# The order of the setup in a linear-attention and mixture-of-experts kernel

## The chip, the cores and the metric

The kernel runs on one core of a Trainium2 chip. The metric is the device time of one execution in microseconds. TensorE multiplies (and turns matrices), VectorE, ScalarE and GpSimd do elementwise work, SyncE issues most DMAs. Each engine works through its own instructions in order and waits for the others by semaphores.

## The reference

For each of 4 batches and 8 heads (width 48) a linear attention with decay w and a bonus u runs over 768 steps. Its rows of 8 x 48 = 384 then go through a mixture of 8 experts, one per token.

```python
for t in range(S):                                   # S = 768
    kt, vt, rt = (k[:, :, t], v[:, :, t], r[:, :, t])
    cur = np.einsum('bhd,bhe->bhde', u[None] * kt, vt)
    y[:, :, t] = np.einsum('bhd,bhde->bhe', rt, state + cur)
    state = w[None, :, :, None] * state + np.einsum('bhd,bhe->bhde', kt, vt)
...
logits = x @ w_gate + modality_bias[modality_id]     # x: 3072 rows of 384
e_idx = np.argmax(logits, axis=1)                    # gate_w: its softmax probability
h = np.maximum(x[mask] @ w1[e], 0.0)                 # for each expert e, mask = e_idx == e
out[mask] = gate_w[mask, None] * (h @ w2[e])
```

## The kernel before

The attention is cut into 24 units: 6 chunks of 128 steps for each of 4 batches, the batches in the inner order, so units 0 to 3 are the first chunks and have no state behind them. Heads go in 4 pairs of 96 rows. For a unit, `decay` multiplies r with powers of w (tile rc, GpSimd), `keys` multiplies k with inverse powers (kc, VectorE), `scores` multiplies the two on TensorE (32 small products into two banks psc), `causal` masks the two banks (VectorE), `values` multiplies the masked scores with v (py) and makes the state products (pst, kt times v), and `bonus` gives for every row the sum of u, r and k (d, from rk: `own_turned` or `own_keys`), by which `own` scales v (dv, eight activations on ScalarE). `token` adds dv to py, and the rows are scaled, split and turned for the routing. r and k of a unit lie turned in HBM (tile ud, 96 rows; k's half is loaded for some units only). For the units in `TURNED`, k is loaded in rows alone (tile kv) and turned on TensorE (`keys_turned`, tile pkT). `carry` scales k for the state (kt, GpSimd).

The order on every engine is written out by hand: the instructions of an engine run in the order in which `setup` and the loop of `run` name them (`tc.manual_schedule`). PSUM has four banks for scores and turned keys, taken in turn, two for py, one (tag "s") for the state products and the bonus: the state products of a unit can't be written before ScalarE has copied out the state (`state`) and d (`taken`) of the unit before.

`setup` makes powers of w: w (1.5 KB, loaded first by SyncE) is spread on VectorE and summed up by a scan into the table pw; ScalarE and VectorE write powk and powr from it, each in halves. Unit 0's k is multiplied by VectorE in two pieces, r by GpSimd (pairs 0 and 1, one by one) and by VectorE (pairs 2 and 3). Rows 0 to 15 of the tiles ud, kv and kt, and the state tiles, are blanked: ud0 by VectorE, ud1 by GpSimd, ud2, ud3, kt and st[1] by ScalarE. u is loaded into single elements of a tile of 96 x 4 (uT) and copied by GpSimd into ub. wtok holds the decays that `carry` uses: four wk on ScalarE, turned on TensorE. Ten products of ones (pwarm, `WARM`) are issued before the first scores, and three more (`DENSE`) in front of unit 1's scores, whose banks are written over by them. All loads are issued by SyncE. After setup, step 0 of the loop in `run` starts with unit 1's scores; `setup2` (the gate's weights, the biases) is spread over the first steps, one instruction at a time.

Of the kernel before, what the change touches and what calls it, by code (L numbers as in the profile page):

```python
# [49 lines left out]
GROUPED = 6  # L50
# [13 lines left out]
LOW, TOP = 64 - D, 64 + D  # L64
HALVES = slice(0, 64), slice(64, TOP)


class _Kernel:
# [16 lines left out]
    def setup(self):  # L85

        nc, c = self.nc, self.c
        w = c.tile([P, NPR], F32, name="w")
        nc.vector.memset(w, 1.0)
        nc.sync.dma_start(w[LOW:TOP, :], self.wT.rearrange("j d a -> (j d) a"))  # L90
        uT = c.tile([P, NPR], F32, name="uT")
        self.ud = [c.tile([P, 2 * NPR * P], F32, name=f"ud{q}") for q in range(4)]
# [3 lines left out]
        zero = c.tile([P, P // 2], F32, name="zero")  # L96
        nc.vector.memset(zero, 0.0)
        warm = self.warm = c.tile([P, 512], F16, name="warm")
        nc.gpsimd.memset(warm, 1.0)
        self.ones16 = warm[:, :P]  # L100
        for t in self.kv:
            nc.vector.memset(t[:, :LOW], 0.0)
        nc.vector.memset(self.ud[0][:LOW], 0.0)
        nc.gpsimd.memset(self.ud[1][:LOW], 0.0)
        H2 = P // 2
        blank = lambda t: nc.scalar.copy(t.rearrange("p (a z) -> p a z", z=P // 2), zero[: t.shape[0]].unsqueeze(1).to_broadcast([t.shape[0], t.shape[1] // (P // 2), P // 2]))
        self.tables = c.tile([P, 3, NPR, H2 + 1], F32, name="tables")
        wb, one0, pw = (self.tables[:, q] for q in range(3))
# [4 lines left out]
        nc.vector.memset(one0[:, :, 0:1], 1.0)  # L113
        nc.vector.memset(uT, 0.0)
        blank(self.ud[2][:LOW])
        self.turned(0)
        self.turned(1)
        nc.sync.dma_start(uT[LOW:TOP, :], self.u.rearrange("o (a z) -> z (o a)", a=NPR))
        self.lines(1, 0)
# [3 lines left out]
        for i in range(3):  # L123
            self.lines(i, 1)
        wg = c.tile([P, DC * E], F32, name="wgf")
        nc.sync.dma_start(wg, self.wg)
        bias = c.tile([P, 2 * E], F32, name="bias")
        nc.sync.dma_start(bias, self.bias.to_broadcast([P, 2 * E]))
        mod = c.tile([P, 2 * NT // P], I32, name="mod")
        nc.sync.dma_start(mod, self.mod)  # L130
        self.raw_in = wg, bias, mod


        pt = self.ps_a.tile([P, 512], F32, tag="big", name="pwarm")
        for _ in range(WARM):
            nc.tensor.matmul(pt, self.ones16, warm, start=True, stop=True)


        self.ones = c.tile([P, P], F32, name="ones")
        nc.vector.memset(self.ones, 1.0)  # L140
        id32 = self.id32 = c.tile([P, P], F32, name="id32")
        make_identity(nc, id32)
        self.mask = c.tile([P, P], F32, name="mask")
        nc.gpsimd.affine_select(self.mask, self.ones, pattern=[[1, P]], compare_op=ALU.is_gt, fill=0.0, base=0, channel_multiplier=-1)
        self.counts()
        flat = lambda t: t.rearrange("p a z -> p (a z)")
# [14 lines left out]
        p64 = pw[:, :, H2 : H2 + 1].rearrange("p a o -> p (a o)")  # L161
        nc.vector.tensor_mul(self.w128, p64, p64)
        self.ub, self.uw = (c.tile([P, NPR, 2], F32, name=n) for n in ("ub", "uw"))
        self.decay(0, NPR, NPR // 2)
        self.keys(0, 2)
        u = self.ctx_[0]
        nc.vector.tensor_mul(u["rc"][:TOP, NPR // 2 :], u["rT"][:TOP, NPR // 2 :], self.powr[:TOP, NPR // 2 :])
        self.own_turned(0)
        self.decay(1)
        self.scores(0)  # L170
        self.wtok = c.tile([P, NPR, 2 * D], F32, name="wtok")
        wk = []
        for pr in range(NPR):
            t = self.a.tile([P, P], F32, tag="wk", name=f"wk{pr}", bufs=4)
            nc.scalar.activation(t, powk[:, pr, :], AF.Copy, scale=self.w128[:, pr : pr + 1])
            wk.append(t)
        blank(self.ud[3][:LOW])
        for t in self.kt:
            nc.scalar.copy(t[:, :, :LOW], zero[:, : NPR * LOW].rearrange("p (a z) -> p a z", a=NPR))
        pt = self.ps_y.tile([P, 512], F32, tag="y", name="pwk")  # L180
        for pr in range(NPR):
            nc.tensor.transpose(pt[:, pr * P : (pr + 1) * P], wk[pr], id32)
        nc.scalar.copy(self.wtok, pt.rearrange("p (a z) -> p a z", a=NPR)[:, :, LOW:TOP])
        blank(self.st[1].rearrange("p b a e -> p (b a e)"))
# [67 lines left out]
    def counts(self):  # L252

        c, v = self.c, self.nc.gpsimd
        self.onesb = c.tile([P, P], BF16, name="onesb")
        v.memset(self.onesb, 1.0)
        self.id16 = c.tile([P, P], F16, name="id16")
        make_identity(self.nc, self.id16)
        self.tok = c.tile([P, NT // P], I32, name="tok")
# [7 lines left out]
        self.base = c.tile([P, E], F32, name="base")  # L267
        v.tensor_copy(self.base, self.cbase)
        self.line = c.tile([P, 1], F32, name="line")
        v.tensor_copy(self.line, self.tok[:, 0:1])  # L270

# [56 lines left out]

    def turned(self, i):
# [5 lines left out]
        self.nc.sync.dma_start(ud[LOW:TOP, :m], self.pd[b * NCH + c].rearrange("j d n -> (j d) n")[:, :m])  # L335
        self.ctx_.setdefault(i, {}).update( rT=ud[:, :n].rearrange("p (a t) -> p a t", a=NPR), kT=ud[:, n:].rearrange("p (a t) -> p a t", a=NPR))
# [55 lines left out]

    def own_turned(self, i):

        u = self.ctx_[i]
        u["rk"], u["uw"] = self.a.tile([P, NPR, P], F32, tag="rk", name=f"rk{i}"), self.ub
        self.nc.vector.tensor_mul(u["rk"][:TOP], u["kT"][:TOP], u["rT"][:TOP])

    def keys(self, i, n=1):
        nc, a, u = self.nc, self.a, self.ctx_[i]  # L400
        u["kc"] = a.tile([P, NPR, P], F32, tag="kc", name=f"kc{i}")
        for q in range(n):
            s = slice(q * NPR // n, (q + 1) * NPR // n)
            nc.vector.tensor_mul(u["kc"][:TOP, s], u["kT"][:TOP, s], self.powk[:TOP, s])

# [34 lines left out]
    def scores(self, i):  # L440
        nc, u = self.nc, self.ctx_[i]
        u["ps"] = [self.ps_a.tile([P, 512], F32, tag="big", name=f"psc{i}_{j}") for j in range(2)]
        if i == 1:

            for q in range(DENSE // 2):
                nc.tensor.matmul(u["ps"][q % 2], self.ones16, self.warm, start=True, stop=True)

        for pr in range(NPR):
            for q in range(2):
                s = slice(64 * q, 64 * q + 64)  # L450
                for j, r in enumerate(HALVES):
                    nc.tensor.matmul(u["ps"][j][s, pr * P : (pr + 1) * P], u["kc"][r, pr, s], u["rc"][r, pr, :], start=True, stop=True)  # L452
# [712 lines left out]
    def run(self):  # L1165
        nc, tc, m = self.nc, self.tc, self.m
# [233 lines left out]
        i, j = NU - 2, NU - 1  # L1400
# [208 lines left out]
```

## Time and profile before

| | us |
|---|---|
| median of 3 runs | 334.5 |
| lowest, highest | 333.94, 335.64 |
| profiled execution, its own time | 336.65 |
| its span | 334.6 |
| TensorE busy in it | 320.0 (96%) |
| VectorE, ScalarE, GpSimd busy | 213.5, 181.7, 159.7 |

The profile is of one execution; the span runs from its first to its last instruction. Times of rows are microseconds from the start of the span. A timeline row begins with the start and the length of a group of like instructions, which may overlap the next; the instruction's engine, line, operation, tiles (out<-in), shape and number follow, and in brackets the idle time of the engine before it with what ended that. PEld is the load of TensorE's stationary operand, SPq the issuing of DMAs by SyncE.

### The profile page before, as it was taken

The numbers are of one execution on the slowest core, as the hardware profiler recorded it, in microseconds if no ns is written. First come the engines' busy times: TensorE is split into PE (matmuls) and PEld (weight loads), VectorE is DVE, ScalarE is ACT, GpSimd is POOL, SyncE is SP. The second block draws the span as 40 slices with busy tenths as digits, with TensorE's granted clock in tenths as the row PEclk, the third lists the DMA queues.
The fourth block names the chain that finished last, engine by engine and source line by source line (L and its number), as shares of the span: only waits on it lengthen the run. The fifth ranks groups of instructions, "written<-read, shape, count | busy, mean of one in ns | idle before, by whom it ended". The sixth has DMA issues, their size and how long they took to land. (4 is left out here: it accounts for less than half of the span.)

```text
span 334.6 us, 15202 instructions
## 1 busy us (share of the span) xinstructions
PE 320.0 (96%) x5434; PEld 263.5 (79%) x5434; DVE 213.5 (64%) x727; ACT 181.7 (54%) x500; POOL 159.7 (48%) x241
## 2 busy tenths in 40 slices
PE   7999998998999999999999999999999999999992
PEld 2888897898978888797878788886888877777771
DVE  6878985899988988896667422286333332234950
ACT  7898888789655578676422222274222225543820
POOL 8978863967599886554458212203111111111211
PEclk9999999899999999999999999999999999999999
DMA  6879986995579999954246431119512211122110
GB/s 185 244 171 207 204 250 222 293 229 155 126 197 270 267 223 299 275 156 119 78 106 231 156 78 47 47 47 332 121 50 65 50 47 24 47 56 62 37 47 5
DMA packets 58013, 48.71 MB, mean 146 GB/s; under 512 B 42344, under 2 KB 50807, under 8 KB 57712
## 3 DMA queue, kind: packets, MB, share of 16 engines
q1 hardware_dynamic: 54768, 38.63, 47.5%
q0 software_dynamic: 3200, 9.47, 8.2%
q8 instruction: 30, 0.49, 0.7%
q14 instruction: 15, 0.12, 0.1%
HBM read 27.99 MB, written 11.83 MB: 119 GB/s over the span
## 5 line engine op out<-in xcount | busy, mean ns | idle before, releaser
L1067 PEld LDWEIGHTS <-whi 128*128 128x128 f16 x1248 | 72.6, 98 | 3.6 <-issue 0.7
L1076 DVE SCALAR_TENSOR_TENSOR hl<-phb,hh 128x256 f16<-128x256 f32 (+1 forms) x48 | 24.4, 508 | 66.8 <-ACTq L1540 66.8
L1130 PEld LDWEIGHTS <-hh 128*128 128x128 f16 x416 | 39.1, 98 | 25.3 <-ACT hh L1071 1.2
L1067 PE MATMUL phb<-mxT,whi 128*128 128x128 f16 x768 | 50.7, 219 | 0.0
L438 ACT ACTIVATE dv<-kv,d 128x48 f32<-128x48 f32 x172 | 43.0, 325 | 0.0
L1071 ACT ACTIVATE hh<-phb 128x256 f16<-128x256 f32 (+1 forms) x48 | 21.5, 455 | 32.4 <-PE phb L1067 22.9
L1067 PEld LDWEIGHTS <-wlo 128*128 128x128 f16 x624 | 37.8, 98 | 0.0
L1036 POOL TENSOR_TENSOR seenb<-otb,putb 128x1 int32<-128x1 int32 x16 | 4.1, 257 | 63.0 <-ACTq L1540 50.8
L458 DVE TENSOR_TENSOR at<-psc,mask 128x512 f32<-128x512 f32 x48 | 32.5, 681 | 1.5 <-PE psc L452 1.4
L1130 PEld LDWEIGHTS <-hl 128*128 128x128 f16 x208 | 19.8, 98 | 15.7 <-issue 2.5
L366 POOL TENSOR_TENSOR rc<-ud,powr 112x512 f32<-112x512 f32 (+1 forms) x25 | 30.8, 1237 | 0.2
L1027 ACT ACTIVATE otb<-po,fac 128x384 f32<-128x384 f32 x16 | 9.3, 580 | 39.5 <-PE phb L1067 39.5
L452 PE MATMUL psc<-rc,kc 64*64 64x128 f32 (+1 forms) x768 | 28.5, 281 | 1.2 <-POOL rc L366 1.0
L701 POOL DMA_INDIRECT rows<-row,posi x24 | 24.6, 1026 | 10.2 <-issue 3.6
L1067 PE MATMUL phb<-mxT,wlo 128*128 128x128 f16 x384 | 29.3, 219 | 0.0
L1130 PE MATMUL po<-whi,hl 128*128 128x384 f16 x136 | 28.0, 326 | 1.2 <-PEq L1605 0.7
L1130 PE MATMUL po<-whi,hh 128*128 128x384 f16 x136 | 27.7, 326 | 0.6 <-ACT hh L1071 0.4
L489 PE MATMUL py<-kv,at 128*64 128x48 f32 x768 | 27.0, 222 | 1.2 <-issue 1.2
L1067 PE MATMUL phs<-mxT,whi 128*128 128x128 f16 x432 | 27.3, 219 | 0.6 <-issue 0.6
L1130 PE MATMUL po<-wlo,hh 128*128 128x384 f16 x136 | 27.7, 326 | 0.0
L452 PEld LDWEIGHTS psc<-rc,kc 64*64 64x64 f32 (+1 forms) x768 | 21.9, 135 | 6.5 <-issue 2.5
L489 PEld LDWEIGHTS py<-kv,at 128*64 128x64 f32 x768 | 25.3, 138 | 2.1 <-issue 1.8
(292 smaller groups left out, 625.6 us busy)
## 6 DMA issues: line engine op xcount, KB each, us to landing
kv<-in_pt SPq DMA_DIRECT2D x21, 384.0 KB, 4.8
ud<-in_pd SPq DMA_DIRECT2D x14, 384.0 KB, 5.4
raw<-in_w SPq DMA_DIRECT2D x12, 256.0 KB, 5.1
raw<-in_w SPq DMA_DIRECT2D x6, 512.0 KB, 5.2
raw<-in_w SPq DMA_DIRECT2D x2, 1536.0 KB, 6.5
rows<-pad SPq DMA_DIRECT2D x10, 193.0 KB, 3.6
ud<-in_pd SPq DMA_DIRECT2D x10, 192.0 KB, 3.8
rt<-in_pt SPq DMA_DIRECT2D x7, 192.0 KB, 5.2
```

The lines of the kernel that those rows point to most:

```text
L366: nc.gpsimd.tensor_mul(u["rc"][:TOP, s], u["rT"][:TOP, s], self.powr[:TOP, s])
L438: nc.scalar.activation(u["dv"][:, sl], u["v"][:, sl], AF.Copy, scale=u["d"][:, h : h + 1])
L452: nc.tensor.matmul(u["ps"][j][s, pr * P : (pr + 1) * P], u["kc"][r, pr, s], u["rc"][r, pr, :], start=True, stop=True)
L458: nc.vector.tensor_mul(u["at"][:, j * NPR : (j + 1) * NPR, :], u["ps"][j].rearrange("p (q t) -> p q t", q=NPR), self.mask.unsqueeze(1).to_ ...
L489: nc.tensor.matmul(py[t, sl], u["at"][:, j * NPR + pr, t], u["v"][:, sl], start=c == h == 0, stop=h == H - 1, skip_group_check=True)
L701: i = nc.gpsimd.indirect_dma_start(out=self.rows, out_offset=bass.IndirectOffsetOnAxis(ap=u["posi"][:, b : b + 1], axis=0), in_=u["row"][: ...
L1027: self.nc.scalar.activation(ot, po[:, :DM], AF.Copy, scale=gf[:, t : t + 1])
L1036: i1 = nc.gpsimd.tensor_tensor(seen, ot[:, 0:1].bitcast(I32), idx, ALU.add)
L1067: self.nc.tensor.matmul(ph[:, q * P : (q + 1) * P], w[:, c0 : c0 + P], self.xT[:, xq, t * P : (t + 1) * P], start=i == q == 0, stop=i == l ...
L1071: self.nc.scalar.activation(self.hh[:, f0 : f0 + fb, t * P : (t + 1) * P], p3, AF.Relu)
L1076: self.nc.vector.scalar_tensor_tensor(self.hl[:, f0 : f0 + fb, r], p3, 0.0, self.hh[:, f0 : f0 + fb, r], ALU.max, ALU.subtract)
L1130: self.nc.tensor.matmul(po[:, :DM], h[:, f, t * P : (t + 1) * P], w[:, c0 : c0 + DM], start=first, stop=last)
```

## The change

- Unit 0's load of r and k is issued by ScalarE; the others stay with SyncE. The loads of wg, bias and mod go behind unit 3's and 4's.
- u is loaded as four rows of 96 (ux), turned by TensorE (one transpose of four columns) and copied into ub by two copies on ScalarE.
- ud0's rows and kt's are blanked by ScalarE early, ud2's by GpSimd; the blanks of ud3 and st[1] on ScalarE move behind `taken(0)`.
- `first` gives the first products of unit 0 in pieces in another order (VectorE: k of pairs 0 and 1, r of pairs 0 and 1, w128, k of pairs 2 and 3, r of pair 2; GpSimd: r of pair 3), and the first scores go through the pairs in the order 0, 1, 3, 2.
- rk of unit 0 is multiplied by GpSimd, behind unit 1's decay, instead of VectorE.
- `keys(1)` stands between unit 0's two masks; `keys_turned(2)` is in the setup; the bonus of unit 0 comes behind it.
- GpSimd's constants are split: `numbers` early, `masks` behind rk, `counts` behind the carry of unit 1.
- Nine products of ones at the start instead of ten, none in front of unit 1's scores.

```diff
-WARM = 10
+WARM = 9
-DENSE = 6
...
+        self.turned(0, nc.scalar)
+        self.turned(1)
+        ux = c.tile([NPR, TOP], F32, name="ux")
+        self.ub, self.uw = (c.tile([P, NPR, 2], F32, name=n) for n in ("ub", "uw"))
+        nc.gpsimd.memset(ux, 0.0)
+        nc.gpsimd.memset(self.ub, 0.0)
+        nc.sync.dma_start(ux[:, LOW:], self.u.rearrange("o (a z) -> (o a) z", a=NPR))
         for t in self.kv:
             nc.vector.memset(t[:, :LOW], 0.0)
-        nc.vector.memset(self.ud[0][:LOW], 0.0)
         nc.gpsimd.memset(self.ud[1][:LOW], 0.0)
...
-        nc.vector.memset(uT, 0.0)
-        blank(self.ud[2][:LOW])
-        self.turned(0)
-        self.turned(1)
-        nc.sync.dma_start(uT[LOW:TOP, :], self.u.rearrange("o (a z) -> z (o a)", a=NPR))
+        blank(self.ud[0][:LOW])
+        for t in self.kt:
+            nc.scalar.copy(t[:, :, :LOW], zero[:, : NPR * LOW].rearrange("p (a z) -> p a z", a=NPR))
         self.lines(1, 0)
...
-        nc.vector.memset(self.ones, 1.0)
+        nc.gpsimd.memset(self.ones, 1.0)
...
-        self.counts()
+        nc.gpsimd.memset(self.ud[2][:LOW], 0.0)
+        self.numbers()
...
-        nc.vector.tensor_mul(self.w128, p64, p64)
-        self.ub, self.uw = (c.tile([P, NPR, 2], F32, name=n) for n in ("ub", "uw"))
-        self.decay(0, NPR, NPR // 2)
-        self.keys(0, 2)
-        u = self.ctx_[0]
-        nc.vector.tensor_mul(u["rc"][:TOP, NPR // 2 :], u["rT"][:TOP, NPR // 2 :], self.powr[:TOP, NPR // 2 :])
-        self.own_turned(0)
+        self.first(p64)
         self.decay(1)
+        self.own_turned(0, nc.gpsimd)
         self.scores(0)
...
-        blank(self.ud[3][:LOW])
-        for t in self.kt:
-            nc.scalar.copy(t[:, :, :LOW], zero[:, : NPR * LOW].rearrange("p (a z) -> p a z", a=NPR))
+        self.masks()
+        psd = self.ps_s.tile([P, 512], F32, tag="s", name="psd")
+        nc.tensor.transpose(psd[:TOP, :NPR], ux, id32[:NPR, :NPR])
+        for j, r in enumerate(HALVES):
+            nc.scalar.copy(self.ub[r, :, j], psd[r, :NPR])
+        self.keys_turned(1)
         pt = self.ps_y.tile([P, 512], F32, tag="y", name="pwk")
         for pr in range(NPR):
             nc.tensor.transpose(pt[:, pr * P : (pr + 1) * P], wk[pr], id32)
         nc.scalar.copy(self.wtok, pt.rearrange("p (a z) -> p a z", a=NPR)[:, :, LOW:TOP])
+        self.causal(0, 0)
+        self.keys(1)
+        self.causal(0, 1)
+        self.own_turned(1)
+        self.keys_turned(2)
+        self.bonus(0, psd)
+        self.taken(0)
+        blank(self.ud[3][:LOW])
         blank(self.st[1].rearrange("p b a e -> p (b a e)"))
-        nc.gpsimd.memset(self.ub, 0.0)
-        for j, r in enumerate(HALVES):
-            nc.gpsimd.tensor_copy(self.ub[r, :, j], uT[r])
-        self.keys_turned(1)
-        self.causal(0, 0)
-        self.causal(0, 1)
-        self.keys(1)
-        self.own_turned(1)
         self.carry(0)
         self.decay(2)
         nc.gpsimd.tensor_mul(self.uw, self.ub, w.unsqueeze(2).to_broadcast([P, NPR, 2]))
-        pst = self.ps_s.tile([P, 512], F32, tag="s", name="psd")
-        self.bonus(0, pst)
-        self.taken(0)
         self.carry(1)
+        self.counts()
         self.feed(3)
...
+    def first(self, p64):
+
+        nc, u, half = self.nc, self.ctx_[0], NPR // 2
+        u["rc"] = self.a.tile([P, NPR, P], F32, tag="rc", name="rc0", bufs=4)
+        u["kc"] = self.a.tile([P, NPR, P], F32, tag="kc", name="kc0")
+        part = lambda eng, out, x, pw, s: eng.tensor_mul(u[out][:TOP, s], u[x][:TOP, s], pw[:TOP, s])
+        lo, hi = slice(0, half), slice(half, NPR)
+        part(nc.gpsimd, "rc", "rT", self.powr, slice(NPR - 1, NPR))
+        part(nc.vector, "kc", "kT", self.powk, lo)
+        part(nc.vector, "rc", "rT", self.powr, lo)
+        nc.vector.tensor_mul(self.w128, p64, p64)
+        part(nc.vector, "kc", "kT", self.powk, hi)
+        part(nc.vector, "rc", "rT", self.powr, slice(half, NPR - 1))
...
-        if i == 1:
-
-            for q in range(DENSE // 2):
-                nc.tensor.matmul(u["ps"][q % 2], self.ones16, self.warm, start=True, stop=True)
-
-        for pr in range(NPR):
+        for pr in range(NPR) if i else (0, 1, 3, 2):
...
-            if i < GROUPED:
+            if 0 < i < GROUPED:
                 each(i + 2, self.keys_turned)
```

## Rows read from the trace of the kernel before

**Rows 1.** Timeline of TensorE, 0 to 27 us (start, length, group)

```profile
1.38 4.45 PE L136 MATMUL pwarm<-warm 128*128 128x512 f16 x10 [1.38 <-POOL warm L99]
...
6.40 0.45 PE L452 MATMUL psc<-rc,kc 64*64 64x128 f32 x8 [0.56 <-POOL rc L366]
7.25 0.89 PE L452 MATMUL psc<-rc,kc 64*64 64x128 f32 x24 [0.41 <-POOL rc L366]
...
9.09 0.63 PE L413 MATMUL psd<-ub,rk 112*64 112x2 f32 x16
...
10.14 0.81 PE L446 MATMUL psc<-warm 128*128 128x512 f16 x3
10.88 1.10 PE L452 MATMUL psc<-rc,kc 64*64 64x128 f32 x32
...
22.85 1.33 PE L489 MATMUL py<-kv,at 128*64 128x48 f32 x32
24.32 0.58 PE L502 MATMUL pst<-kv,kt 128*64 128x48 f32 x15
```

**Rows 2.** Timeline of ScalarE over the same time

```profile
4.86 0.41 ACT L159 COPY powr<-powk 128x256 f32<-128x256 f32 x1
...
6.35 1.03 ACT L106 COPY ud<-zero 16x1024 f32<-16x1024 f32 x1
7.28 0.68 ACT L179 COPY kt<-zero 128x64 f32<-128x64 f32 x4
...
9.14 1.48 ACT L106 COPY st<-zero 128x1536 f32<-128x1536 f32 x1
10.51 0.17 ACT L421 COPY d<-psd 128x8 f32<-128x8 f32 x1
10.72 1.91 ACT L438 ACTIVATE dv<-kv,d 128x48 f32<-128x48 f32 x8
12.54 0.21 ACT L212 ACTIVATE wgsq<-wgf 128x24 f32<-128x24 f32 x1
...
14.00 0.64 ACT L544 COPY st<-pst 64x192 f32<-64x192 f32 x2 [1.16 <-PE pst L413]
...
23.20 0.32 ACT L229 ACTIVATE wghl<-wgf,wgs 128x24 f16<-128x24 f32 x1 [0.51 <-DVE wgs L318]
...
24.06 0.17 ACT L421 COPY d<-pst 128x8 f32<-128x8 f32 x1
```

**Rows 3.** Timeline of VectorE over the same time

```profile
2.98 0.23 DVE L147 COPY tables<-w 128x256 f32<-128x256 f32 x1
...
4.93 0.76 DVE L404 TENSOR_TENSOR kc<-ud,powk 112x256 f32<-112x256 f32 x2
...
21.83 0.62 DVE L566 SCALAR_TENSOR_TENSOR row<-py,sx,row 128x384 f16<-128x384 f32 x1 [1.73 <-ACT row L562]
...
22.43 0.68 DVE L458 TENSOR_TENSOR at<-psc,mask 128x512 f32<-128x512 f32 x1
```

**Rows 4.** Tenths of a microsecond: busy time by engine, clock, DMA share, GB/s

```profile
2.20:2.30 0.10, 0.10 (x2) 0.09 (x1) 0.10 (x2) 0.10 (x1) 0.10 (x2) 1.00 0.16 4
...
2.50:2.60 0.10, 0.10 (x1) 0.00 (x0) 0.10 (x2) 0.10 (x1) 0.10 (x1) 1.00 2.88 369
```

**Rows 5.** Timeline of SyncE's DMA issues: the loads of units 0 and 1

```profile
1.44 0.88 SPq L335 DMA_DIRECT2D ud<-in_pd  x2
```

**Rows 6.** GpSimd by line and shape, 5.6 to 8.5 us (busy, mean ns)

```profile
L366 POOL TENSOR_TENSOR rc<-ud,powr 112x128 f32<-112x128 f32 x2 | 1.5, 768 | 0.0
L366 POOL TENSOR_TENSOR rc<-ud,powr 112x512 f32<-112x512 f32 x1 | 1.3, 1265 | 0.0
```

**Rows 7.** Timeline of GpSimd: the copy that the change moves

```profile
4.95 0.46 POOL L268 COPY base<-idxf 128x8 f32<-128x8 f32 x1
```

**Rows 8.** Busy time by engine (TensorE first) and granted clock, two later stretches

```profile
53.50:54.75 1.25, 0.08 (x3) 0.03 (x2) 0.00 (x0) 1.25 (x3) 0.00 (x0) 1.00 0.89 325
57.00:61.00 4.00, 4.00 (x59) 3.56 (x60) 2.55 (x10) 3.96 (x13) 3.77 (x5) 0.57 0.80 228
```

More of the change, by code (lines that the diff above doesn't have):

```diff
@@ L90, in setup @@
         nc.sync.dma_start(w[LOW:TOP, :], self.wT.rearrange("j d a -> (j d) a"))
-        uT = c.tile([P, NPR], F32, name="uT")
         self.ud = [c.tile([P, 2 * NPR * P], F32, name=f"ud{q}") for q in range(4)]
@@ L124, in setup @@
             self.lines(i, 1)
[L125 to L131, printed above, removed]
         pt = self.ps_a.tile([P, 512], F32, tag="big", name="pwarm")
@@ L195, in setup @@
         nc.gpsimd.tensor_mul(self.uw, self.ub, w.unsqueeze(2).to_broadcast([P, NPR, 2]))
-        pst = self.ps_s.tile([P, 512], F32, tag="s", name="psd")
-        self.bonus(0, pst)
-        self.taken(0)
         self.carry(1)
+        self.counts()
         self.feed(3)
+        wg = c.tile([P, DC * E], F32, name="wgf")
+        nc.sync.dma_start(wg, self.wg)
         self.turned(4)
+        bias = c.tile([P, 2 * E], F32, name="bias")
+        nc.sync.dma_start(bias, self.bias.to_broadcast([P, 2 * E]))
+        mod = c.tile([P, 2 * NT // P], I32, name="mod")
+        nc.sync.dma_start(mod, self.mod)
+        self.raw_in = wg, bias, mod
+    def first(self, p64):
[10 more added lines that the diff above has]
+        part(nc.vector, "rc", "rT", self.powr, slice(half, NPR - 1))
     def setup2(self):
@@ L254, in counts, with masks @@
         c, v = self.c, self.nc.gpsimd
+        self.base = c.tile([P, E], F32, name="base")
+        v.tensor_copy(self.base, self.cbase)
+        self.line = c.tile([P, 1], F32, name="line")
+        v.tensor_copy(self.line, self.tok[:, 0:1])
+    def masks(self):
+        c, v = self.c, self.nc.gpsimd
         self.onesb = c.tile([P, P], BF16, name="onesb")
@@ L258, in counts, with numbers @@
         make_identity(self.nc, self.id16)
+    def numbers(self):
+        c, v = self.c, self.nc.gpsimd
         self.tok = c.tile([P, NT // P], I32, name="tok")
@@ L266, in counts @@
         self.idx, self.rev, self.cbase = (ci[:, q] for q in range(3))
[L267 to L270, printed above, removed]
     def setup5(self):
@@ L327, in feed, with turned @@
         self.lines(i)
-    def turned(self, i):
+    def turned(self, i, by=None):
         b, c = self.units[i]
@@ L334, in turned @@
         m = n if i in TURNED else 2 * n
-        self.nc.sync.dma_start(ud[LOW:TOP, :m], self.pd[b * NCH + c].rearrange("j d n -> (j d) n")[:, :m])
+        (by or self.nc.sync).dma_start(ud[LOW:TOP, :m], self.pd[b * NCH + c].rearrange("j d n -> (j d) n")[:, :m])
         self.ctx_.setdefault(i, {}).update( rT=ud[:, :n].rearrange("p (a t) -> p a t", a=NPR), kT=ud[:, n:].rearrange("p (a t) -> p a t", a=NPR))
@@ L359, in pace, with decay @@
         self.nc.values_load(ap[:1].bitcast(I32)[:, :1], engines=SP, skip_runtime_bounds_check_because="the value is not used, only the time at which it is there")
-    def decay(self, i, n=1, of=None):
+    def decay(self, i):
         nc, u = self.nc, self.ctx_[i]
         u["rc"] = self.a.tile([P, NPR, P], F32, tag="rc", name=f"rc{i}", bufs=4)
-        for q in range(of or n):
-            s = slice(q * NPR // n, (q + 1) * NPR // n)
-            nc.gpsimd.tensor_mul(u["rc"][:TOP, s], u["rT"][:TOP, s], self.powr[:TOP, s])
+        nc.gpsimd.tensor_mul(u["rc"][:TOP], u["rT"][:TOP], self.powr[:TOP])
     def carry(self, i):
@@ L391, in own_keys, with own_turned, keys @@
         nc.gpsimd.tensor_mul(u["rk"][:TOP], u["rc"][:TOP], u["kc"][:TOP])
-    def own_turned(self, i):
+    def own_turned(self, i, by=None):
         u = self.ctx_[i]
         u["rk"], u["uw"] = self.a.tile([P, NPR, P], F32, tag="rk", name=f"rk{i}"), self.ub
-        self.nc.vector.tensor_mul(u["rk"][:TOP], u["kT"][:TOP], u["rT"][:TOP])
-    def keys(self, i, n=1):
+        (by or self.nc.vector).tensor_mul(u["rk"][:TOP], u["kT"][:TOP], u["rT"][:TOP])
+    def keys(self, i):
         nc, a, u = self.nc, self.a, self.ctx_[i]
         u["kc"] = a.tile([P, NPR, P], F32, tag="kc", name=f"kc{i}")
-        for q in range(n):
-            s = slice(q * NPR // n, (q + 1) * NPR // n)
-            nc.vector.tensor_mul(u["kc"][:TOP, s], u["kT"][:TOP, s], self.powk[:TOP, s])
+        nc.vector.tensor_mul(u["kc"][:TOP], u["kT"][:TOP], self.powk[:TOP])
     def bonus(self, i, pst):
```

## The prediction

> **What bounds the kernel now.** I read the table of slices first: TensorE is busy in nine tenths or more of nearly all of them, only the first slice and the last are thinner. So a setup that lets TensorE start earlier should shorten everything behind it, if TensorE is what the next microseconds wait for. That is not visible in a mean, so I read the timeline of TensorE over the first 27 us, then those of ScalarE and VectorE beside it.
>
> TensorE [rows 1]: ten products that write nothing useful fill 1.38 to 5.83. The first scores start at 6.40 and again at 7.25, each time released by GpSimd's decayed r, and end at 8.14. Then it runs on without a gap (transposes, the bonus products at 9.09, three more idle products at 10.14, unit 1's scores at 10.88). From these rows alone the setup is bound by the road to the first scores.
>
> ScalarE [rows 2] tells another story. It waits once, 1.16 us, until the first state is there at 14.00, and from there it works without a gap until it waits 0.51 for VectorE at 23.20: copies of state, the scalings by d, the squares, and pieces of the second setup. At 24.06 it copies d of unit 3 out of the one bank of the state products, which ends at 24.23; TensorE's next group into that bank starts at 24.32, though its group before (22.85) would have let it go on earlier: it took 1.33 us, spread out. VectorE shows the same dependence [rows 3]: it stands still for 1.73 us until ScalarE's row at 21.83, and only then does unit 3's second mask (22.43, done 23.1) come, which TensorE's group of 22.85 needs for its odd heads. So by 24 us TensorE has been caught up by ScalarE and VectorE. A lead won at 8 us is worth something at 24 us only if ScalarE's chain starts earlier too. That chain goes back through 14.00 to d of unit 0 and to what ScalarE does next to it.
>
> **The change part by part.**
>
> *Road to the first scores.* The chain starts with w: VectorE copies it at 2.98, works up the powers, and has kc of unit 0 from 4.93 on (two pieces, 0.76) [rows 3]; ScalarE writes the last quarter of the powers for r at 4.86 to 5.27 [rows 2]. Taking a blank of 16 rows from VectorE (1.03 for the like one on ScalarE, [rows 2]) gains little: w's bytes moved until 2.3 [rows 4], so it lands between 2.3 and 2.98, and ScalarE now starts with a load's issue (0.44, half of SP's two, [rows 5]) and has the four small blanks of kt (0.68, [rows 2]) ahead of the powers too, where it waited before. Bounds: 0.1 gained to 0.3 lost; I take 0, since the powers' last piece hangs on VectorE's, and that on w. Then VectorE's first piece of rc (as long as one of kc, 0.4) ends at about 5.7 and pairs 0 and 1 start at 5.8 instead of 6.40; pair 3 needs GpSimd's single piece (0.77 beside a busy VectorE, [rows 6]: 5.3 to 6.1) and the second kc (6.25); pair 2 the last rc (6.45). The scores end at about 6.95 instead of 8.14: 1.2 us of lead. GpSimd must reach its piece by 5.3: before, everything ahead of the copy at 4.95 was done by then [rows 7]; the change adds a blank of 16 rows (about 1) and takes out three small operations of the masks there and the two copies behind it, so it gets there between 4.95 and 5.95, and I take 5.3.
>
> *Between the two scores.* Before, unit 1's scores started 10.88 − 8.14 = 2.74 after the first ended, the last 0.74 (10.14 to 10.88) being the three products that write nothing. Without them TensorE has four groups of transposes and the bonus (0.63, [rows 1]). But the bonus needs rk of unit 0, and that product moves from VectorE to GpSimd, behind decay(1): both are 112x512 products of 1.27 [rows 6], the first stretched by about 0.2 while VectorE reads the same memory. 6.1 + 1.45 + 1.27 = 8.8. So the bonus runs 8.85 to 9.45, and unit 1's scores start at 9.4 to 9.5: TensorE leads by 1.4 to 1.5 there. keys(1) between the two masks, the transposes of u (one of four columns in place of a small DMA of single elements, GpSimd's two copies and a memset) and the later wg, bias and mod cost nothing: VectorE has its third product of that stretch done at about 9.0, ScalarE waits for the bonus anyway, and wg is first read at 12.54 [rows 2], some 6 us after its new issue. The one warm product less (0.43) lies in time in which TensorE waits.
>
> *Where the lead goes.* After the change ScalarE's order is: d of unit 0, blank of ud3, blank of st, the eight scalings of unit 0, the square of wg, then the state copies that stood at 14.00. Before, both blanks were done ahead of d. From start to next start [rows 2]: d 0.2 (10.51 to 10.72), ud3's blank 0.93 (6.35 to 7.28), st's blank 1.37 (9.14 to 10.51), scalings 1.82 (10.72 to 12.54), the square 0.2 to 0.3. Sum 4.5 to 4.6. With the bonus ending at 9.45, d starts at about 9.55, and the state copies at 9.55 + 4.55 = 14.1, against 14.00 now. The 1.16 us in which ScalarE waited are filled by blanks that stood where it had to wait for something else anyway (new waits: about 0.6 for w128, which now comes behind the first rc, so the four wk start at 5.9; 0.6 for wk's transposes; 0.9 for the bonus). Behind 14.00 ScalarE's and VectorE's order is the old one and has no room, so the second mask of unit 3 (22.43) and d of unit 3 (24.06) come 0.1 later than now, and TensorE, ahead by 1.4 us until then, waits at unit 3's values for 1.5 us and goes on at 24.32 + 0.1. GpSimd, which now has rk of unit 0 (1.27) and the two copies (0.46 and less, [rows 7]) behind its first pieces, is up to 1.2 later from 13 us on; TensorE, which would meet it, is itself held until 24.4.
>
> *The load of unit 0 on ScalarE's queue.* Until now w was alone: unit 0's bytes began at 2.5, w's had moved by 2.3 [rows 4]. Now unit 0's 384 KB are issued by an engine with nothing ahead of them, some 0.6 before the 1.44 of [rows 5], and their first bytes come at about 1.9, ahead of w's. From below: w is not disturbed, 0. From above: w waits until they are through, at the 0.9 that they take beyond 2.3 (384 KB from 1.9 at some 300 GB/s, an estimate below the 369 of [rows 4], end at 3.2). I take 0.1, because w is only 1.5 KB; every microsecond of it goes through powers, rk, bonus and d to ScalarE's chain one to one. *By the Trainium skill (DMA: Bandwidth & Descriptors, "Queues, rings and completion order") the queues of SP and ACT share the same 16 DMA engines, which take turns between them by whole packets, and a completion signal lands only behind all earlier writes of its engine, whatever the queue; by that rule w's signal comes behind whatever of unit 0 is already on its way, a few tenths, and the sum would be 0.3 to 0.5 worse than mine. No row of the trace before shows two such queues at once.*
>
> **The sum.** Profiled execution: 336.65 us, of which the span is 334.6; the median of the other runs is 334.5. Change at 24.3 us: +0.1 (ScalarE's chain) + 0.1 (w) = +0.2; behind it the work and its order are the old ones, so the end moves by as much: 336.85 in the profiled frame, 334.7 against the median.
>
> **The rivals.**
>
> *The lead is kept (gain).* If the state copies at 14.00 come earlier than I work out, because GpSimd's rk is ready by 8.2 and the blanks run shorter beside idle neighbours, or if TensorE is held by something at 24 us that moves with it. For it: 1.4 us of lead at unit 1's scores. Against it: the rows at 21.83 to 24.32. It gives 334.5 − 1.5 = 333.0, and 332.4 if the first scores get the full 1.9 of the gaps and idle products together.
>
> *TensorE's clock falls (slower).* My forecast makes TensorE wait about 1.5 us in one piece at 21.7 to 23.2. The trace has one such place [rows 8]: TensorE was busy 0.08 of 1.25 us from 53.50, and from 57 to 61 its granted clock is 0.57 of full in the mean, so for most of that at the lower of its two levels, 1.2 instead of 2.4 GHz. That is 0.43 x 4 = 1.7 us of its work lost. Before the change nothing of that length stands ahead of 50 us. [...] The price is 1.7 at most, and 1.1 if a third of it falls into waits that TensorE has anyway: 335.8 to 336.4.
>
> *w comes late.* With 0.6 to 0.9 in place of 0.1, everything from the powers on is later and 335.2 to 335.5 results. This is the rival of the shared queues above. For it: w's chain has no slack; against it: its size.
>
> **How the numbers follow.** What a measurement of this kernel can tell from no change is about 0.5%, 1.67 us (333.94 to 335.64 before). Chances: ScalarE's chain unchanged 0.47 (334.7, from 333.9 to 335.5), lead kept 0.25 (333.0), clock falls 0.18 (336.0), w late 0.10 (335.3). Faster than 332.83: half of the second and some of the first's edge, 0.19. Slower than 336.17: four tenths of the clock case, edges of the others with it, 0.14. Between: 0.67. Range for 8 in 10: 332.8 to 336.4, which reaches into the kept lead at one end and to the upper price of the clock at the other.
>
> **What would show it.** Right: first scores at 5.8, unit 1's scores at 9.4 to 9.5, no idle products, but ScalarE's state copies at 14.0 to 14.3, both blanks between d and the scalings, a new wait of TensorE of over 1 us ahead of 23.2, and its state products of unit 3 still at about 24.4. Wrong: state copies of unit 0 before 13.4, or TensorE's unit 3 ended by 23.5 (the lead is kept); VectorE's copy of w later than 3.3 (the queue); a granted clock of one half between 23 and 30 us (the clock).

## The result and the profile after

The changed kernel takes 338.67 us (median of 6 runs, 337.72 and up) against 334.72 of the kernel before: 1.011 of its time, interval 1.0085 to 1.0136. By that ratio it is slower by 3.7 us (2.8 to 4.6). The forecast was no change. Comparisons below use undisturbed executions only, so a median over all runs can lie above what a ratio says; the trace of experiment 7 is disturbed, and only its first 4 us are read.

The profiled execution takes 337.72 us with a span of 335.7. That is only 1.1 over the span of before: from unit 3's state products to the end it takes 307.7, before's 310.3, which has a lower clock at 57 to 61 us [rows 8] where this one has none. So I compare by landmarks in the first 30 us, not by spans.

VectorE of the changed kernel, then GpSimd, from 4.4 us on (columns as in [rows 1]):

```profile
4.44 0.29 DVE L143 COPY tables<-w 128x256 f32<-128x256 f32 x1 [2.58 <-DMA w<-in_wT]
...
7.12 0.42 DVE L212 TENSOR_TENSOR w<-tables 128x4 f32<-128x4 f32 x1
7.47 0.41 DVE L207 TENSOR_TENSOR kc<-ud,powk 112x256 f32<-112x256 f32 x1
7.80 1.36 DVE L207 TENSOR_TENSOR rc<-ud,powr 112x128 f32<-112x128 f32 x1
```

```profile
6.84 0.69 POOL L207 TENSOR_TENSOR rc<-ud,powr 112x128 f32<-112x128 f32 x1 [1.99 <-ACT powr L155]
7.49 1.53 POOL L385 TENSOR_TENSOR rc<-ud,powr 112x512 f32<-112x512 f32 x1
8.97 1.32 POOL L416 TENSOR_TENSOR rk<-ud 112x512 f32<-112x512 f32 x1
```

and the DMA engines in three half microseconds (last column GB/s):

```profile
1.50:2.00 0.50, 0.50 (x2) 0.17 (x2) 0.28 (x2) 0.50 (x1) 0.50 (x1) 1.00 0.60 90
2.00:2.50 0.50, 0.50 (x2) 0.15 (x1) 0.00 (x0) 0.50 (x1) 0.50 (x3) 1.00 0.66 180
2.50:3.00 0.50, 0.50 (x2) 0.15 (x1) 0.00 (x0) 0.49 (x2) 0.42 (x4) 1.00 0.82 328
```

Unit 0's bytes move from 1.84 us on (the first row is empty up to there; the forecast was 1.9), at 180 GB/s until 2.5; before, there was next to nothing at 2.2 [rows 4]. VectorE stands still for 2.58 us until w is there and copies it at 4.44; before, it was busy until 2.98 and did not wait [rows 3]. Its last piece, a quarter of r, takes 1.36 and ends at 9.16, just behind GpSimd's product of 7.49 (9.02). TensorE follows:

```profile
1.39 4.02 PE L131 MATMUL pwarm<-warm 128*128 128x512 f16 x9 [1.39 <-POOL warm L97]
7.26 1.21 PE L464 MATMUL psc<-rc,kc 64*64 64x128 f32 x24 [1.85 <-DVE rc L207]
9.21 0.54 PE L464 MATMUL psc<-rc,kc 64*64 64x128 f32 x8 [0.74 <-DVE rc L207]
...
9.87 1.10 PE L375 MATMUL pkT<-id,kv 128*112 128x128 f32 x4
...
12.60 0.73 PE L430 MATMUL psd<-ub,rk 112*64 112x2 f32 x16
...
26.15 0.32 PE L501 MATMUL py<-kv,at 128*64 128x48 f32 x4 [0.84 <-DVE row L578]
26.81 1.02 PE L501 MATMUL py<-kv,at 128*64 128x48 f32 x28 [0.34 <-DVE wgs L339]
27.97 0.58 PE L514 MATMUL pst<-kv,kt 128*64 128x48 f32 x15
```

Three things are to be seen. TensorE idles 1.85 ahead of the first scores (0.56 before, [rows 1]). The first four transposes behind the scores take 1.10; the like four took 0.66 in the kernel before:

```profile
8.07 0.66 PE L182 MATMUL pwk<-id,wk 128*128 128x128 f32 x4
```

And the landmark of the forecast, unit 3's state products, comes at 27.97 instead of 24.32 [rows 1]: 3.65 later, close to the 3.7 of the runs. The windows (columns as in [rows 4]: TensorE busy first, its clock the last but two) say why the transposes are long:

```profile
9.00:10.00 1.00, 0.79 (x10) 0.51 (x11) 0.30 (x2) 0.00 (x0) 1.00 (x2) 0.72 1.05 309
10.00:11.00 1.00, 1.00 (x6) 1.00 (x7) 0.55 (x1) 0.32 (x2) 0.86 (x4) 0.50 0.94 249
...
12.00:13.00 1.00, 1.00 (x14) 0.66 (x14) 1.00 (x3) 0.34 (x1) 0.58 (x1) 0.57 0.32 65
```

The granted clock is 0.50, the lower of the two levels, from 9.4 to nearly 12.9 us. ScalarE has the order that was forecast:

```profile
13.38 0.17 ACT L438 COPY d<-psd 128x8 f32<-128x8 f32 x1 [1.05 <-PE psd L430]
13.45 1.04 ACT L110 COPY ud<-zero 16x1024 f32<-16x1024 f32 x1
14.39 1.47 ACT L110 COPY st<-zero 128x1536 f32<-128x1536 f32 x1
15.77 1.91 ACT L455 ACTIVATE dv<-kv,d 128x48 f32<-128x48 f32 x8
17.58 0.20 ACT L225 ACTIVATE wgsq<-wgf 128x24 f32<-128x24 f32 x1
...
17.79 0.62 ACT L556 COPY st<-pst 64x192 f32<-64x192 f32 x2
...
27.71 0.17 ACT L438 COPY d<-pst 128x8 f32<-128x8 f32 x1
```

From d to the state copies it takes 4.41 (forecast 4.55), and it works from there to the wait ahead of 26.85 and to unit 3's d as before. So the chain was read rightly; it starts 3.7 late.

### The profile page after: what moved, and what is told of

Its sections match the earlier page's. It is cut to its first block, busy times and chain, and to the rows that moved or that the text cites. A ratio compares the mean times of both kernels' runs of the same rounds, so it can differ in the third digit from the quotient of the medians.

```text
span 335.7 us, 15200 instructions
## 1 busy us (share of the span) xinstructions
PE 318.3 (95%) x5431; PEld 262.4 (78%) x5431; DVE 213.7 (64%) x724; ACT 181.9 (54%) x502; POOL 162.0 (48%) x242
## 5 line engine op out<-in xcount | busy, mean ns | idle before, releaser
L464 PE MATMUL psc<-rc,kc 64*64 64x128 f32 (+1 forms) x768 | 27.7, 276 | 3.2 <-DVE rc L207 2.6
L713 POOL DMA_INDIRECT rows<-row,posi x24 | 25.4, 1057 | 10.3 <-issue 3.3
L385 POOL TENSOR_TENSOR rc<-ud,powr 112x512 f32<-112x512 f32 x23 | 29.7, 1293 | 0.2
L1021 DVE SCALAR_TENSOR_TENSOR wlo<-raw,ws,whi 128x1024 f16<-128x1024 f32 (+1 forms) x20 | 25.9, 1319 | 1.4 <-issue 0.7
```

The source lines that it names most:

```text
L385: nc.gpsimd.tensor_mul(u["rc"][:TOP], u["rT"][:TOP], self.powr[:TOP])
L713: i = nc.gpsimd.indirect_dma_start(out=self.rows, out_offset=bass.IndirectOffsetOnAxis(ap=u["posi"][:, b : b + 1], axis=0), in_=u["row"][: ...
L1021: self.nc.vector.scalar_tensor_tensor(self.wlo[:, sl], self.raw[:, sl], sc, self.whi[:, sl], ALU.mult, ALU.subtract)
```

## The experiments

Each was run in five rounds beside the kernel before. The table has the landmarks of each kernel's one profiled execution: starts, but for the end of unit 0's scores and for the length of the first four transposes behind them. The last column is its time over that of before.

| kernel | w copied | scores end | four transposes | d | state copies | unit 3's state products | ratio (interval) |
|---|---|---|---|---|---|---|---|
| before | 2.98 | 8.14 | 0.66 | 10.51 | 14.00 | 24.32 | 1 |
| after | 4.44 | 9.75 | 1.10 | 13.38 | 17.79 | 27.97 | 1.011 (1.0085–1.0136) |
| 1 load by SyncE | 2.65 | 8.49 | 1.10 | 11.99 | 16.40 | 26.58 | 1.0082 (1.0053–1.0110) |
| 2 blanks ahead of d | 4.36 | 9.85 | 1.10 | 13.56 | 16.55 | 26.88 | 1.0068 (1.0033–1.0102) |
| 3 both | 2.65 | 8.16 | 0.65 | 10.77 | 13.78 | 24.10 | 0.9992 (0.9963–1.0021) |
| 4 fourteen ones | 4.46 | 9.68 | 0.65 | 11.89 | 16.29 | 26.46 | 1.0045 (1.0012–1.0079) |
| 5 old, load ahead | 4.40 | 9.64 | 1.11 | 12.48 | 16.26 | 26.57 | 1.0143 (1.0086–1.0200) |
| 6 old, blanks behind d | 2.98 | 7.65 | 0.66 | 9.65 | 14.05 | 24.23 | 1.0015 (0.9986–1.0044) |
| 8 best try | 2.68 | 7.97 | 1.10 | 11.82 | 14.39 | 24.71 | 0.9948 (0.9912–0.9984) |
| 9 r in one piece | 4.58 | 9.54 | 1.10 | 12.89 | 17.29 | 27.47 | 1.0080 (1.0052–1.0107) |
| 10 best, twelve ones | 2.64 | 7.51 | 0.65 | 10.91 | 13.36 | 23.55 | 0.9966 (0.9937–0.9994) |
| 11 old, nine ones, no idle products | 2.98 | 8.83 | 1.11 | 11.66 | 14.76 | 25.09 | 0.9999 (0.9963–1.0035) |

For after and for 1 to 4, 6 and 9 to 11 the shift of unit 3's state products and that of the time agree to 0.8 us or less. For 5 and 8 they do not. From that landmark to the end the traces take 307.5 (3) to 312.0 us (6), so the span of one trace says little.

**1. Unit 0's load by SyncE again.**

```diff
-        self.turned(0, nc.scalar)
+        self.turned(0)
```

> The changed kernel with unit 0's load issued by SyncE behind w's, as before; all else as changed. In the trace of the changed kernel VectorE waited 2.58 us for w and copied it at 4.44 (2.98 before); ScalarE's first state copies came at 17.79 (14.00 before), TensorE's state products of unit 3 at 27.97 (24.32). Theory Q (the load ahead of w is the first cause): w copied by 3.0, first scores at 5.8, and TensorE's wait between its ones and the first scores falls from 1.85 to about 0.4, so that its clock may hold; state copies at 14.5 to 15.5, state products of unit 3 at 25 to 26; about 335.5, 2.5 to 3 us under the changed kernel, still 0.5 to 1.5 over the kernel before. Rival B (only the blanks behind d count): w on time, but state copies stay within 0.7 of 17.8, 338. Rival C (only the clock, by the idle products left out): w on time, clock still at half in the setup, state copies at 16.3 to 17, 337.

```profile
2.65 0.29 DVE L143 COPY tables<-w 128x256 f32<-128x256 f32 x1 [0.80 <-DMA w<-in_wT]
...
6.38 1.35 DVE L207 TENSOR_TENSOR rc<-ud,powr 112x128 f32<-112x128 f32 x1
```

w comes 1.79 earlier and everything up to d 1.3 to 1.4 earlier. But most of the slowdown stays, as rival C had it (state copies at 16.40): the last piece of r takes 1.35 as it did, and the clock is at half. The queue alone is not the cause.

**2. Only the two blanks moved back ahead of d.**

```diff
+        blank(self.ud[3][:LOW])
+        blank(self.st[1].rearrange("p b a e -> p (b a e)"))
         for j, r in enumerate(HALVES):
             nc.scalar.copy(self.ub[r, :, j], psd[r, :NPR])
...
         self.taken(0)
-        blank(self.ud[3][:LOW])
-        blank(self.st[1].rearrange("p b a e -> p (b a e)"))
```

> The changed kernel with the blanks of ud3 and st[1] on ScalarE ahead of the two copies of u instead of behind d of unit 0; unit 0's load still by ScalarE. Theory (w's lateness and the blanks add up on ScalarE's chain): w at 4.4, d of unit 0 at 13.4 as in the changed kernel, the scalings right behind it, state copies no longer 4.4 behind d but as soon as TensorE's bonus of unit 1 is done (16.3 in the changed kernel): 16.35, unit 3's state products at 26.5, 1.4 us under the changed kernel, about 337.2. Rival Q alone (the late w moves TensorE and that bounds everything): no change, 338.5. Rival B (only the blanks): 2.3 us less, 336.3.

```profile
16.55 0.64 ACT L556 COPY st<-pst 64x192 f32<-64x192 f32 x2 [0.67 <-PE pst L430]
```

With d as late as after's, the state copies come 1.24 earlier, and the products of unit 3 1.09. Here TensorE is what they wait for (0.67 at 16.55). So where d is late, the blanks behind it cost 1.1 to 1.2.

**3. Both of these.**

```diff
-        self.turned(0, nc.scalar)
+        self.turned(0)
...
+        blank(self.ud[3][:LOW])
+        blank(self.st[1].rearrange("p b a e -> p (b a e)"))
         for j, r in enumerate(HALVES):
```

> The changed kernel with both: unit 0's load by SyncE behind w, and the two blanks ahead of the copies of u. Theory: w by 3.0, scores of unit 0 done by about 8.3 (VectorE's last piece of rc still slow beside GpSimd), bonus of unit 0 done at 10.6, unit 1's scores from 10.6, state copies at 13.7 to 14.0: within 0.5 us of the kernel before, 334.3. If only the load counts, as the first of these runs; if something else of the change costs time behind 20 us (order of loads, GpSimd's later queue), over 335.5 though the state copies come by 14.0.

```profile
7.71 0.45 PE L464 MATMUL psc<-rc,kc 64*64 64x128 f32 x8 [0.67 <-DVE rc L207]
```

As fast as before: 0.9992. From these last scores on its TensorE is at full speed (transposes 0.65), unlike that of 1 with the same work (0.70 for these eight, then 1.10). Its nine ones ahead of them are at half (4.02, as in after).

**4. Fourteen products of ones instead of nine.**

```diff
-WARM = 9
+WARM = 14
```

> The changed kernel with 14 products of ones at the start instead of 9, which fill TensorE's wait of 1.85 us ahead of the first scores (5.41 to 7.26); load and blanks as changed. Rival C (the clock, lost because TensorE stood still ahead of the first scores and the idle products are left out, is what costs): the granted clock stays full from 7 to 13 us, the transposes and the bonus take 2.5 instead of 3.6 us, d of unit 0 at 12.3, state copies at 16.7: 1.1 us less, 337.5. Theory Q: w is as late as in the changed kernel, at 4.4, and at least 2.5 us of the 3.7 remain. If the clock has no part: no change, 338.5.

```profile
7.28 1.21 PE L464 MATMUL psc<-rc,kc 64*64 64x128 f32 x24 [1.29 <-DVE rc L207]
9.23 0.45 PE L464 MATMUL psc<-rc,kc 64*64 64x128 f32 x8 [0.74 <-DVE rc L207]
...
9.75 0.65 PE L375 MATMUL pkT<-id,kv 128*112 128x128 f32 x4
```

The first scores start as late as after's, and the rest of the setup runs at the higher level: d 1.49 earlier, state copies 1.50. This is the price of the clock in the trace, and the time is shorter too (1.0045 for 1.011, the intervals apart).

**5. The kernel before, with only unit 0's load issued by ScalarE.**

```diff
+        self.turned(0, nc.scalar)
...
-        self.turned(0)
```

> The kernel before with one thing of the change: unit 0's load issued by ScalarE ahead of w. Theory Q (a load of 384 KB on the other queue ahead of w makes w late, and the chain from w to ScalarE's state copies has no slack): VectorE copies w at 4.3 to 4.5 instead of 2.98; first scores near 7.9, a gap behind the ten products of ones of 2 us, after which TensorE may run at half clock; state copies at 15.4 (clock full) to 16.9 (half); 1.5 to 3 us over the kernel before. Rival (w was late in the changed kernel for another reason, as the loads of u or unit 1 issued earlier): w as before, no difference.

```profile
4.40 0.29 DVE L147 COPY tables<-w 128x256 f32<-128x256 f32 x1 [1.34 <-DMA w<-in_wT]
```

This one part slows the old kernel by as much as the whole change, within the intervals: w 1.42 later, a gap of 2.33 behind the ones, the clock at half, state products of unit 3 2.25 later. That is 2.25 of the 4.8 us by which it is slower; the traced execution is the fastest of its six (337.56 of up to 342.41), and where the others lose the rest no row tells.

**6. The kernel before, with only the blanks behind d.**

```diff
-        blank(self.ud[3][:LOW])
...
-        blank(self.st[1].rearrange("p b a e -> p (b a e)"))
...
         self.taken(0)
+        blank(self.ud[3][:LOW])
+        blank(self.st[1].rearrange("p b a e -> p (b a e)"))
```

> The kernel before with another thing of the change: the blanks of ud3 and st[1] on ScalarE behind d of unit 0. Theory: d at 9.8 instead of 10.51, then two blanks and the scalings, state copies at 9.8 + 4.5 = 14.3 instead of 14.0, TensorE's state products of unit 3 0.3 later: 0.3 over the kernel before, not to be told from it. So the blanks cost only where d is late. Rival (the blanks cost their whole length, whatever d does): 2.3 us over it.

```profile
9.65 0.17 ACT L421 COPY d<-psd 128x8 f32<-128x8 f32 x1 [0.89 <-PE psd L413]
9.71 1.04 ACT L106 COPY ud<-zero 16x1024 f32<-16x1024 f32 x1
10.66 1.47 ACT L106 COPY st<-zero 128x1536 f32<-128x1536 f32 x1
...
14.05 0.62 ACT L544 COPY st<-pst 64x192 f32<-64x192 f32 x2
```

No cost: d comes 0.86 earlier, the blanks fill the slack, and the state copies are where they were. This is the forecast's picture of the blanks, alone.

**7. In the changed kernel, w issued by ScalarE right ahead of unit 0's load.**

```diff
-        nc.sync.dma_start(w[LOW:TOP, :], self.wT.rearrange("j d a -> (j d) a"))
+        nc.scalar.dma_start(w[LOW:TOP, :], self.wT.rearrange("j d a -> (j d) a"))
```

> The changed kernel with w issued by ScalarE too, right ahead of unit 0's load: the same queue, but w first. If the order is what counts (w's bytes and its completion behind those of unit 0): w copied by 2.8, as with both by SyncE, state copies near 16.4 at half clock or 15.0 at full, 335.5 to 338. If the second queue itself is slow or slows the other: w copied at 4 or later, 338.5.

```profile
3.54 0.79 DVE L143 COPY tables<-w 128x256 f32<-128x256 f32 x1 [1.68 <-DMA w<-in_wT]
```

Missed, in a way that helped: SyncE, with w gone from its list, issued unit 1's 192 KB at 0.81, ahead of w at 0.98. So w was first on its queue and still came late. With 0, 192 and 384 KB issued ahead of it by the other engine, w is copied at 2.65, 3.54 and 4.44: 0.9 us for each 192 KB, by one trace each. By the DMA packets of these traces the last bytes of w move at 2.30, 2.92 and 3.60. The ratio is 1.0112 (1.0051 to 1.0173), so the time gains nothing: unit 0's load now stands behind unit 1's.

**8. The changed kernel with the load by SyncE, r of pairs 2 and 3 in one piece by GpSimd, and each blank where ScalarE waits anyway, ahead of d.**

```diff
-        self.turned(0, nc.scalar)
+        self.turned(0)
...
-        part(nc.gpsimd, "rc", "rT", self.powr, slice(NPR - 1, NPR))
+        part(nc.gpsimd, "rc", "rT", self.powr, hi)
...
-        part(nc.vector, "rc", "rT", self.powr, slice(half, NPR - 1))
```

> The changed kernel with three things mended: unit 0's load by SyncE behind w; r of pairs 2 and 3 by GpSimd in one piece, so that VectorE has no piece of r (1.36 us in the changed kernel for 128 columns, beside GpSimd's 512 of unit 1) in front of the last scores; on ScalarE the blank of ud3 behind the copies of u and that of st[1] behind wtok, both ahead of d. Theory: scores of unit 0 done at 7.0 to 7.4 (8.16 in the run with both, 9.75 in the changed kernel), bonus of unit 0 at 9.1 to 9.6, state copies at 12.8 to 13.2, unit 3's state products at 23.2 to 23.5: 0.8 to 1.2 us under the kernel before, near 334. Rival (VectorE's slow piece costs nothing because rk on GpSimd ends no earlier): bonus at 10.1, state copies at 13.8, level with the run with both.

```profile
5.45 0.89 POOL L207 TENSOR_TENSOR rc<-ud,powr 112x256 f32<-112x256 f32 x1
5.68 0.68 DVE L212 TENSOR_TENSOR w<-tables 128x4 f32<-128x4 f32 x1
5.81 2.16 PE L463 MATMUL psc<-rc,kc 64*64 64x128 f32 x32 [0.41 <-DVE rc L207]
...
24.71 0.58 PE L513 MATMUL pst<-kv,kt 128*64 128x48 f32 x15
```

Faster than both kernels: 0.9948, 1.7 us (0.5 to 3.0) under before. Its landmarks missed what was expected: in its profiled execution the setup ran at half clock, and unit 3's state products come 0.39 later than before's. So this trace doesn't show where the gain lies.

**9. The changed kernel with only that r in one piece** (the second edit of 8).

> The changed kernel with r of pairs 2 and 3 multiplied by GpSimd in one piece (as in the best try, 0.89 us there) and no piece of r on VectorE; the load of unit 0 and the blanks stay as changed. Theory (VectorE's last piece, 1.36 us beside GpSimd, is worth about 0.9 us of the path by itself): scores of unit 0 end at 8.8 to 9.0 instead of 9.75, d and the state copies 0.9 earlier (12.5 and 16.9), 337.8; if the closed gap also holds TensorE's clock, 1.5 more, 336.3. Rival (the piece is hidden, since rk on GpSimd or the copies on ScalarE decide when the bonus starts): state copies at 17.8 again, 338.7.

```profile
7.41 0.67 PE L463 MATMUL psc<-rc,kc 64*64 64x128 f32 x16 [2.08 <-DVE rc L207]
8.45 1.09 PE L463 MATMUL psc<-rc,kc 64*64 64x128 f32 x16 [0.37 <-DVE kc L207]
```

A part: d and the state copies come 0.5 earlier, 0.64 counted from w, which is 0.14 later here. The second sixteen scores could start 0.76 earlier than the last eight did, but run at half clock (1.09 against 0.67 for the first). The gain in time (1.0080 against 1.011) is inside the intervals.

**10. Number 8 with twelve products of ones.**

```diff
-WARM = 9
+WARM = 12
```

> The best try (load by SyncE, r in one piece, blanks ahead of d) with twelve products of ones instead of nine, so that TensorE's gap ahead of the first scores (0.41) closes. Theory (the half clock costs 1.5 us of the setup and the ones hold it): four transposes take 0.65 instead of 1.10, state copies at 12.9 to 13.3 instead of 14.39, 332.5. Rival (ScalarE's and VectorE's chains give nothing back by 24 us, or the clock falls all the same): state products of unit 3 at 24.7 again, 334.0.

```profile
5.99 0.67 PE L463 MATMUL psc<-rc,kc 64*64 64x128 f32 x16
6.84 0.67 PE L463 MATMUL psc<-rc,kc 64*64 64x128 f32 x16 [0.18 <-DVE kc L207]
...
7.58 0.65 PE L374 MATMUL pkT<-id,kv 128*112 128x128 f32 x4
...
23.55 0.58 PE L513 MATMUL pst<-kv,kt 128*64 128x48 f32 x15
...
41.00 0.25 PE L508 MATMUL pst<-st,wd 112*64 112x48 f32 x2 [1.57 <-issue]
```

The setup did what was expected: full clock, state products of unit 3 1.16 earlier than in 8. The time did not: 0.9966, no better than 8. The traced execution lost its lead later, in a pause of 1.57 us at 41 us that nothing in the profile explains ("issue"), with a lower clock behind it. Other executions have such pauses too, at other places [rows 8]. Whether the timed executions of 8 had the full clock, or those of 10 more pauses, one trace of each can't tell.

**11. The kernel before with nine products of ones and none in front of unit 1's scores.**

```diff
-WARM = 10
+WARM = 9
-DENSE = 6
+DENSE = 0
```

> The kernel before with nine products of ones instead of ten and none in front of unit 1's scores; nothing else. Theory A (removing them is free where w comes early): unit 1's scores 0.7 earlier at about 10.15, state copies at 13.3 instead of 14.00 since ScalarE waited 1.16 there, 334.2 to 334.7 against 335. Theory B (these products are what held the clock in the setup): four transposes take 1.10, state copies at 14.8 or later, 336 to 336.5.

```profile
1.39 4.02 PE L136 MATMUL pwarm<-warm 128*128 128x512 f16 x9 [1.39 <-POOL warm L99]
6.41 0.71 PE L452 MATMUL psc<-rc,kc 64*64 64x128 f32 x8 [1.00 <-POOL rc L366]
7.27 1.56 PE L452 MATMUL psc<-rc,kc 64*64 64x128 f32 x24 [0.15 <-POOL rc L366]
8.76 1.11 PE L182 MATMUL pwk<-id,wk 128*128 128x128 f32 x4
```

The trace follows theory B, the time neither (0.9999, where 0.77 us later at unit 3 would be 1.0023, inside the interval). Half speed is there from the first scores on (0.71 against 0.45 for the same eight, [rows 1]), so ahead of the place of the three idle products. What is missing by then is one product of ones; whether that decides it, or the execution, one trace can't tell.

## Why the prediction was wrong

**ScalarE's chain: right.** Both blanks fill the time between d and the scalings, 4.41 instead of 4.55; the state copies set unit 3's state products 10.18 later (10.32 before); TensorE meets its new wait there, though in two pieces (0.84 and 0.34) and without the clock falling. The first scores come 2.82 behind w's copy, as worked out (5.8 − 2.98). GpSimd's order and sizes held: rk ends 10.29, forecast 8.8, late by what its first piece started late (6.84 for 5.3).

The state copies were forecast at 14.1 + 0.1 and came at 17.79, 3.59 later. Three terms make it up, with −0.14 on the blanks:

**1. "I take 0.1, because w is only 1.5 KB": +1.36.** w was copied at 4.44, 1.46 later than before and 1.79 later than with a free road. Even the bound from above, 0.9, was short. It let 384 KB run at 300 GB/s from 1.9 and end at 3.2; by the DMA packets of the trace they ended at 3.56. Not one packet of w's moves before 3.1, where with a free road (1) they move from 2.00 to 2.30; the last one moves at 3.60, and VectorE copies w 0.84 behind it (0.35 in 1). So some 1.30 of the 1.79 are bytes that stood behind unit 0's, and 0.49 lie between the last byte and its use; why these grew no row tells. The size of a small load says nothing of when it is done; what was issued before it does, on whichever queue. Experiments 5 and 7 show this alone and by dose. The rule of the Trainium skill (DMA: Bandwidth & Descriptors, "Queues, rings and completion order") named in the prediction was the better guide: the trace agrees with its order (unit 0's bytes first, then w's), and its price is far above the "few tenths" that I gave it. Its rival had the right mechanism at half the size.

**2. "Pair 2 the last rc (6.45)": +1.34.** Scores took 2.49 from first to last, forecast 1.15. I gave VectorE's last quarter of r some 0.2 (6.25 to 6.45); it took 1.36, because GpSimd works on unit 1's product of 1.53 at the time. I had stretched GpSimd's product by 0.2 for that, and let VectorE's run free. In the five traces with this piece (after, 1 to 4) VectorE's ends 0.14 behind GpSimd's (9.16 and 9.02 after). That it is a wait and not a slower rate, the product of four columns just ahead shows. It is 0.16 long in the kernel before:

```profile
4.74 0.16 DVE L162 TENSOR_TENSOR w<-tables 128x4 f32<-128x4 f32 x1
```

It takes 0.42 after, and 0.68 in experiments 8 and 10 where GpSimd's product beside it is longer (0.89 for 0.69), and ends 0.01 to 0.02 behind it each time. The Trainium skill has it (SBUF — State Buffer, "Who interferes with whom"): a VectorE instruction with two inputs in SBUF contends with a GpSimd instruction that reads SBUF, for a pair of ports that is an exclusive lock; the trace agrees.

**3. "The one warm product less (0.43) lies in time in which TensorE waits": +1.03, the clock.** From the scores' end to d it took 3.63 for 2.6 forecast; at full clock, experiment 4, it takes 2.21. So the clock costs 1.42, of which 0.39 goes to the slack that I had left for GpSimd's rk. I looked for the lower clock at 21.7 to 23.2, where TensorE would wait; it fell at 9.4. Of the seven traces with nine ones six have the transposes at half speed (after, 1, 2, 8, 9, 11; not 3). Of those with ten or more, before, 4, 6 and 10 have them at full; only 5, with w late, has not. So I had priced the dropped products by their time alone and put their clock at nothing, without a reason. But that the dropped one cost the clock here is not shown. Behind the same nine ones the level rises at other places: before the ninth ends in 1 (nine in 3.58), after it in after and 3 (4.02), and in 2, 8 and 11 not even the first scores have it (0.71 for eight in 11, 2.16 for 32 in 8). Nor do the times agree: fourteen for nine help the changed kernel (4), twelve for nine give experiment 8's kernel nothing (10), and nine for ten cost the old one nothing (11). Experiment 3 says that nine can do; what decides it in a given execution stays open.

Sum: 1.36 + 1.34 + 1.03 − 0.14 = 3.59. The parts don't add up when taken out one by one: without the late w (1) unit 3 gains 1.39, without the half clock (4) 1.51, without the blanks behind d (2) 1.09, without VectorE's piece (9) 0.50. Each takes slack that another leaves; 1 and 2 together (3) take away all 3.87, some of it perhaps by the full clock that 3's trace has besides; its time, too, is that of the kernel before.

**The kept lead** is possible, but not with this order: with w early, the clock full, r in one piece and the blanks out of the chain (10) unit 3 comes 0.77 earlier than before, and the time is 1.1 us shorter (0.2 to 2.1), as the rival had it in kind.

**Slips in the working** that bear on nothing above: 334.5 − 1.9 is 332.6, not 332.4. By the chances given, 0.19 lie below 332.83 and 0.14 above 336.17, so the range holds some 7 in 10, not 8. And ScalarE waits more than once ahead of 14.00: also 0.87 at 4.01 and 0.80 at 8.76.

## What to carry to other kernels

A tiny load at the head of a long chain must be issued before every large one, on all queues, and each queue that another engine opens must be checked for what slips ahead. A product split between VectorE and GpSimd has to be timed with them as one resource where both read SBUF: here a quarter of the work waited for nearly all of the neighbour's product. That products which write nothing lie "in time where the engine waits" is no argument for dropping one: what they may be worth is the clock. Whether one more or less matters has to be timed; it did in one case of three here.

## What was not expected of the hardware

- 384 KB issued 0.17 us earlier by another engine (0.81 and 0.98) delayed a load of 1.5 KB by 1.79 us; 192 KB by 0.89. Some 1.30 and 0.62 of these are w's bytes moving later, the rest the way from the last byte to its use.
- A VectorE product of four columns can take 0.68 us beside GpSimd: its length is the rest of GpSimd's instruction.
- The granted clock reads 1.00 in the windows until its first recorded change, even where products run at half speed: the ones of after are 0.43 apart from 1.39 on (4.02 for nine; the last seven of experiment 4's fourteen are 0.22 apart), and experiment 11's four transposes take 1.11 in a stretch that shows 1.00. Durations tell the clock there, the column doesn't. That the level had not yet risen by the first scores of 2, 8 and 11 is read from them alone.
